# Reordering the prologue of a fused attention and two-layer MoE kernel: loads, scores, value sums and first copies

## The chip, the cores and the metric

The kernel runs on one core of a Trainium2 chip. The metric is the device time of one execution in microseconds (us). Three executions of the kernel before took 1382.09, 1383.53 and 1384.44 us; their median, 1383.53 us, is what the changed kernel is compared with. One more execution was recorded by the profiler.

## The reference

Attention with pooled keys and values feeds a dense feed-forward layer with ELU, and that feeds a layer of eight experts of which each token takes one.

```python
k_p = k.reshape(B, H, Sp, pool, D).mean(axis=3)          # B=8, H=8, S=576, D=64, pool=8, Sp=72
v_p = v.reshape(B, H, Sp, pool, D).mean(axis=3)
scores = q @ k_p.T / sqrt(D);  attn = softmax(scores);  x = attn @ v_p      # 4608 tokens x 512
h = x @ w_in;  g = where(h > 0, h, exp(min(h, 0)) - 1);  x = g @ w_out      # 512 -> 2048 -> 512
e = argmax(x @ w_gate);  out = softmax weight * relu(x @ w1[e]) @ w2[e]     # 8 experts, F = 1024
```

## The kernel before, in words

The 4608 tokens are 36 tiles of 128, three tiles to a block, twelve blocks. `first_block` (L867) is the prologue: it makes the attention output of tiles 0 to 2 (block 0). After it comes a list of steps, `step` (L836), one for each block and each of 16 slices of the hidden layer: 12 matmuls of the first product (`g1_mm`, L500, into tile `h`), the ELU on ScalarE and VectorE, and nine matmuls of the second product (`g2`, L540) of two steps earlier. The first steps also prepare tiles 3 to 5 and batch 1's keys (`k_sum`, L352, 40 small matmuls in step 0), and decode the weights.

For one tile t the prologue does this:

- `a_load` (L388) loads the queries `qT`; `s_mm` (L396) writes the scores of four heads into each of two PSUM banks (32 recorded matmuls);
- `s_max` and `s_exp` (L416, L421): VectorE takes the negative maxima `mx`, ScalarE the exponentials, eight per tile, each followed by a read of its accumulated sum `sm`;
- `s_norm` (L428): three VectorE instructions that scale the exponentials `s`;
- `t_mm` (L456): 16 recorded transposes on TensorE into two banks `aTp`; `t_copy` (L466) copies each bank to SBUF as `aT`;
- `pv_mm` (L472): 16 recorded matmuls of `aT` with the pooled values `v`; `pv_copy` (L483) writes the high part `xh` on ScalarE and the low part `xl` on VectorE, and both read the bank.

The pooled values of batch 0 come from `v_sum` (L338): five parts of the loaded values `natv`, two recorded matmuls each, accumulated in one bank, which `v_sum_copy` (L349) copies to `v` on ScalarE. A weight piece (n, c) is loaded by `w_load` (L183), multiplied by `w_mul` (L207), completed by the three VectorE instructions of `w_bits` (L222), and split by `w_hi` (ScalarE, L241) and `w_lo` (VectorE, L244). `warm(n)` (L288) issues n matmuls on zeros whose result nobody reads.

The order on every engine and on SP's DMA queue is the order of the program text, because the prologue and the steps stand inside a manual schedule (L953). PSUM banks are handed out in turn: `bank` (L279) gives alternately one of three banks `y` and one of three banks `a`. So the scores of tiles 0, 1 and 2 take y0/a0, y1/a1, y2/a2; the transposes of tile 0 take y0/a0, those of tile 1 y1/a1; `pv_mm(0)` takes y2, the transposes of tile 2 a2/y0, `pv_mm(1)` a0, `s_mm(3)` y1/a1, and `pv_mm(2)` takes y2 again. A bank is free for its next writer when its last reader is done. `v_sum(0)` and `warm` use two other banks, `h`.

The order of the prologue before, on the three compute engines, from the scores on:

- TensorE: scores 0, warm 6, scores 1, warm 6, scores 2, value parts 0 and 1, transposes 0, parts 2 and 3, transposes 1, part 4, `pv_mm(0)`, transposes 2, `pv_mm(1)`, scores 3, `pv_mm(2)`, step 0.
- ScalarE: exponentials 0, 1, 2, `w_hi(0,0)`, the two copies of `aT` 0, the copy of `v`, the two copies of `aT` 1, `xh` 0, `w_hi(0,1)`, one copy of `aT` 2, `xh` 1, `xh` 2.
- VectorE: maxima 0, `w_mul(0,0)`, maxima 1, `w_bits(0,0)`, maxima 2, `s_norm(0)`, `w_mul(0,1)`, `s_norm(1)`, `s_norm(2)`, `w_bits(0,1)`, `xl` 0, one copy of `aT` 2, `w_lo(0,0)`, `xl` 1, `w_lo(0,1)`, `xl` 2, maxima 3.

Of the kernel before, what the change touches and what calls it, by code (L numbers as in the profile page):

```python
# [97 lines left out]
def fused_kernel(ctx: ExitStack, tc: tile.TileContext, q, k, v, w_in, w_out, w_gate, w1, w2, cst, out):  # L98
    nc = tc.nc
# [83 lines left out]
    def w_load(n, c):  # L183
        kind, i = W_ORDER[n][0], int(W_ORDER[n][1])
        if n < len(W_ORDER) - 1:
            raw = w_tile([P, 512, 2], U32, f"raw{n}_{c}")
        elif c == 0:
            raw = mrpool.tile([P, 512, 2], U32, tag="yr", name=f"raw{n}_{c}")
        else:
            r = (2 * i + c) * P  # L190
            raws[n, c] = []
            for x in range(2):
                t = wgb_tile(f"raw{n}_{c}_{x}").bitcast(U32)
                nc.sync.dma_start(t, wov[r:r + P, 512 * x:512 * (x + 1)])
                raws[n, c].append((slice(256 * x, 256 * (x + 1)), t.rearrange("p (f t) -> p f t", t=2)))
            return
        if kind == "i":
            nc.sync.dma_start(
                raw.rearrange("p (c f) t -> p c (f t)", c=2),
                wiv[2 * c * P:2 * (c + 1) * P, 4 * i * P:4 * (i + 1) * P].rearrange("(c p) f -> p c f", p=P),  # L200
            )
        else:
            r = (2 * i + c) * P
            nc.sync.dma_start(raw.rearrange("p f t -> p (f t)"), wov[r:r + P, :])
        raws[n, c] = [(slice(0, 512), raw)]

    def w_mul(n, c, eng=None):  # L207
        if c == 0:
            kind, i = W_ORDER[n][0], int(W_ORDER[n][1])
            shape = [P, KC, 2 * P] if kind == "i" else [P, 2, DM]  # L210
            (wi if kind == "i" else wo)[i] = [
                w_tile(shape, F32R, f"w{kind}{x}{i}") for x in "hl"
            ]
        if n < 12:
            t = w_tile([P, 512], U32, f"dec{n}_{c}")
        else:
            t = spool.tile([P, S], U32, tag="st", name=f"dec{n}_{c}")[:, :512]
        decs[n, c] = t
        for q, r in raws[n, c]:
            (eng or nc.scalar.mul)(t.bitcast(F32)[:, q], r[:, :, 1].bitcast(F32), 2.0 ** -112)  # L220

    def w_bits(n, c):  # L222
        t = decs[n, c]
        raw = raws.pop((n, c))
        nc.vector.tensor_scalar(t, t, 3, None, op0=ALU.logical_shift_left)  # L225
        for q, r in raw:
            nc.vector.scalar_tensor_tensor(  # L227
                t[:, q], r[:, :, 1], 0x80000000, t[:, q], op0=ALU.bitwise_and, op1=ALU.bitwise_or
            )
        for q, r in raw:  # L230
            nc.vector.scalar_tensor_tensor(  # L231
                t[:, q], r[:, :, 0], 29, t[:, q], op0=ALU.logical_shift_right, op1=ALU.bitwise_or
            )
        if n < len(W_ORDER) - 1:
            w_free(f"raw{n}_{c}")
# [52 lines left out]
    def warm(n):  # L288
        ps = bank_h([P, 512], "warm")
        for _ in range(n):  # L290
            nc.tensor.matmul(ps, ones, zeros, start=True, stop=True)
# [32 lines left out]
    def n_load(b, kind):  # L324
        src = (k if kind == "k" else v)[b].rearrange("(s f) -> s f", f=DM)
        ts = []
        for x in range(2):
            t = w_tile([P, 2, DM], F32, f"nat{kind}{b}_{x}")
            nc.sync.dma_start(t, src[2 * P * x:2 * P * (x + 1), :].rearrange("(c p) f -> p c f", p=P))
            ts += [t[:, 0], t[:, 1]]  # L330
        t = w_tile([S - 4 * P, DM], F32, f"nat{kind}{b}_2")
        nc.sync.dma_start(t, src[4 * P:S, :])
        nats[b, kind] = ts + [t]
# [4 lines left out]
    def v_sum(b, parts):  # L338
        if 0 in parts:
            banks["vs", b] = bank_h([P, DM], f"vsum{b}") if b == 0 else bank([P, DM], f"vsum{b}")  # L340
        ps = banks["vs", b]
        for i in parts:
            t = nats[b, "v"][i]
            n, c = t.shape[0], SUM_AT - P // POOLW * i
            nc.tensor.matmul(ps[:SP], sums[:n, c:c + SP], t, start=i == 0, stop=i == 4)  # L345
        if 4 in parts:
            n_free(b, "v")
# [40 lines left out]
    def a_load(t):  # L388
        if t < 6:
            st = w_tile([P, 4, P], F32, f"qT{t}")  # L390
        else:
            st = ring(apool, [P, 4, P], F32, "qT", 2, f"qT{t}")
        nc.sync.dma_start(st, q[t])
        qTs[t] = st

    def s_mm(t):  # L396
        ss[t] = (
            wide["s"][:, :H * SP].rearrange("p (h s) -> p h s", h=H) if t >= T_TURN else work([P, H, SP], "s", f"s{t}"),
            ring(apool, [P, H], F32, "mx", 3, f"mx{t}"),
            ring(apool, [P, H], F32, "sm", 3, f"sm{t}"),  # L400
        )
        ps = [bank([P, 4, SP], f"sp{t}_{o}") for o in range(2)]
        qT = qTs.pop(t)
        for pr in range(4):
            for q in range(2):
                b = (P * t + HQ * q) // S
                qs = slice(HQ * q, HQ * (q + 1))
                for o in range(2):
                    os = slice(D * o, D * (o + 1))
                    nc.tensor.matmul(ps[o][qs, pr], qT[os, pr, qs], kTs[b % 2][os, pr], start=True, stop=True)  # L410
        for o in range(2):
            banks["s", t, o] = ps[o]
        if t < 6:
            w_free(f"qT{t}")
# [13 lines left out]
    def s_norm(t):  # L428
        s, _, sm = ss[t]
        nc.vector.tensor_scalar(sm, sm, 1e-9, float(POOLW), op0=ALU.add, op1=ALU.mult)  # L430
        nc.vector.reciprocal(sm, sm)
        nc.vector.tensor_mul(s, s, sm.unsqueeze(2).to_broadcast([P, H, SP]))
# [23 lines left out]
    def t_mm(t):  # L456
        s = ss[t][0]
        pss = [bank([P, H, HQ], f"aTp{t}_{q}") for q in range(2)]
        for h in range(H):
            for q in range(2):  # L460
                qs = slice(HQ * q, HQ * (q + 1))
                nc.tensor.transpose(pss[q][:SP, h], s[qs, h], ident[qs, qs])
        for q in range(2):
            banks["t", t, q] = pss[q]
# [402 lines left out]
    def first_block():  # L867
        warm(N_WARM)
        for pr in range(4):
            k_load(0, pr)  # L870
        a_load(0)
        a_load(1)
        for c in range(2):
            w_load(0, c)
        a_load(2)
        nc.sync.dma_start(ident, cst[:, C_ID:C_ID + P])
        nc.sync.dma_start(sums, cst[:, C_SUM:C_ALL])
        n_load(0, "v")
        a_load(3)
        for c in range(2):  # L880
            w_load(1, c)
        n_load(1, "k")
        for c in range(2):
            w_load(2, c)

        def exps(t):
            for hh in range(2):
                s_exp(t, hh)

        def maxs(t):  # L890
            for hh in range(2):
                s_max(t, hh)

        for pr in range(4):
            prep_k(0, pr)
        k_scale(0)
        v_tile(0)
        a_load(4)
        n_load(1, "v")
        s_mm(0)  # L900
        warm(6)
        maxs(0)
        exps(0)
        w_mul(0, 0, nc.vector.tensor_scalar_mul)
        s_mm(1)
        warm(6)
        maxs(1)
        exps(1)
        w_bits(0, 0)
        s_mm(2)  # L910
        v_sum(0, range(2))
        maxs(2)
        exps(2)
        a_load(5)
        s_norm(0)
        t_mm(0)
        v_sum(0, range(2, 4))
        w_hi(0, 0)
        t_copy(0, 0, nc.scalar.copy)
        t_copy(0, 1, nc.scalar.copy)  # L920
        w_mul(0, 1, nc.vector.tensor_scalar_mul)
        s_norm(1)
        t_mm(1)
        v_sum(0, range(4, 5))
        v_sum_copy(0)
        s_norm(2)
        pv_mm(0)
        t_mm(2)
        t_copy(1, 0, nc.scalar.copy)
        t_copy(1, 1, nc.scalar.copy)  # L930
        w_bits(0, 1)
        pv_copy(0)
        w_hi(0, 1)
        pv_mm(1)
        s_mm(3)
        t_copy(2, 0, nc.scalar.copy)
        t_copy(2, 1, nc.vector.tensor_copy)
        w_lo(0, 0)
        pv_copy(1)
        pv_mm(2)  # L940
        w_lo(0, 1)
        pv_copy(2)
        w_free("zeros")
        maxs(3)
        for c in range(2):
            w_load(3, c)
        nc.sync.dma_start(small, cst[:, C_W:C_END])
        load_small()
        for c in range(2):
            w_mul(1, c)  # L950
        copy_small()
# [630 lines left out]
```

## Time and profile before

| what | value |
|---|---|
| median of three executions | 1383.53 us (1382.09 to 1384.44) |
| the profiled execution, its own time | 1385.67 us |
| its span, first to last instruction | 1383.8 us |
| TensorE matmuls busy | 1357.7 us, 98% of the span |
| VectorE, ScalarE, GpSimd busy | 983.7, 772.1, 199.2 us |
| mean granted clock of TensorE | 0.993 of full speed |
| DMA moved | 169.41 MB |

The profiled execution is 2.14 us above the median of the other three, and 1.87 us of its own time lie outside the span. All starts are counted from the first instruction of the span. A busy share of TensorE counts matmuls whose ends are modelled, so full does not mean at its peak.

### The profile page before, as it was taken

To read this page: it belongs to the slowest core of one execution; us is meant where nothing else is said; L and a number is where in the kernel's file an instruction comes from. 1 tells how busy PE (TensorE), PEld (TensorE's weight loads), DVE (VectorE), ACT (ScalarE), POOL (GpSimd) and SP (SyncE) were. 2 spreads that over 40 slices of the span, in tenths; PEclk is the share of its full clock that TensorE was granted. 3 is DMA by queue.
4 is the path that set the end of the run, shared out by engine and by line. 5 is a ranking of instruction groups with operands and counts; after the bars stand their busy time and mean duration, and the time that the engine had idled before them with its cause. 6 is when DMAs were issued, how large, how long until landed. Compare 5 with 4: busy or idle time off the path is not lost.

```text
span 1383.8 us, 23759 instructions
## 1 busy us (share of the span) xinstructions
PE 1357.7 (98%) x8481; PEld 1164.8 (84%) x8482; DVE 983.7 (71%) x2395; ACT 772.1 (56%) x1889; POOL 199.2 (14%) x208
## 2 busy tenths in 40 slices
PE   8999999999999999999999999999999999999996
PEld 5798788888888888888889898988888887878785
DVE  7899979988878878787979786976556533335260
ACT  6777766666667676766666665642333333234251
POOL 0011011101211211111210000111121112112020
PEclk9999999999999999999999999999999999999998
DMA  9157434647353553545561522765664465759360
GB/s 348 62 174 211 134 69 108 69 82 71 76 81 63 93 57 76 68 65 83 73 91 39 63 39 46 160 109 174 137 117 159 145 217 194 259 180 338 129 217 22
DMA packets 109143, 169.41 MB, mean 122 GB/s; under 512 B 15509, under 2 KB 53015, under 8 KB 109016
## 3 DMA queue, kind: packets, MB, share of 16 engines
q1 hardware_dynamic: 91528, 135.45, 39.6%
q0 software_dynamic: 17488, 32.37, 12.0%
q8 instruction: 68, 1.11, 0.4%
q14 instruction: 59, 0.48, 0.2%
HBM read 146.35 MB, written 21.88 MB: 122 GB/s over the span
## 4 chain that ended last, share of the span: by engine, by line
PE 85%; DVE 5%; issue 5%; ACT 3%; DMA 1%; POOL 0%; SPq 0%; POOLq 0%; ACTq 0%; DVEq 0%
PE h L506 25%; PE y L548 25%; PE mhD L1212 13%; PE myD L1247 13%; PE pv L479 2%; PE sp L410 1%; PE zTD L1142 1%; DVE dec L227 1%; DVE dec L231 1%; ACT gh L530 1%; DVE junk L599 1%; PE mhT L1212 1%; ACT dec L220 1%; PE vsum L345 1%; DVE dec L225 1%
## 5 line engine op out<-in xcount | busy, mean ns | idle before, releaser
L548 PE MATMUL y<-woh,gh 128*128 128x512 f32 x576 | 230.6, 400 | 6.4 <-DVE yr L562 2.3
L548 PE MATMUL y<-wol,gh 128*128 128x512 f32 x576 | 226.6, 393 | 0.0
L548 PE MATMUL y<-woh,gl 128*128 128x512 f32 x576 | 226.5, 393 | 0.0
L599 DVE SCALAR_TENSOR_TENSOR junk<-yr,wgb 128x512 bf16<-128x512 f32 x264 | 180.7, 684 | 4.2 <-ACT yr L564 1.3
L506 PE MATMUL h<-xh,wih 128*128 128x384 f32 x768 | 168.5, 341 | 1.5 <-ACT xh L492 1.5
L530 ACT CAST gh<-g 128x384 fp32r<-128x384 f32 x192 | 98.6, 514 | 125.9 <-DVE g L524 107.1
L506 PE MATMUL h<-xl,wih 128*128 128x384 f32 x768 | 166.8, 338 | 0.0
L506 PE MATMUL h<-xh,wil 128*128 128x384 f32 x768 | 165.3, 336 | 0.0
L1225 DVE SCALAR_TENSOR_TENSOR hlD<-mhD,hhD 128x512 fp32r<-128x512 f32 x64 | 44.2, 690 | 161.5 <-ACT hhD L1224 153.5
L523 DVE SCALAR_TENSOR_TENSOR g<-g,th 128x384 f32<-128x384 f32 x192 | 106.3, 554 | 74.0 <-ACT th L518 73.8
L506 PEld LDWEIGHTS h<-xh,wih 128*128 128x128 f32 x768 | 139.3, 189 | 18.0 <-ACT xh L492 2.0
L1224 ACT ACTIVATE hhD<-mhD 128x512 fp32r<-128x512 f32 x64 | 38.4, 601 | 199.3 <-PE myD L1247 183.9
L516 ACT ACTIVATE th<-h 128x384 f32<-128x384 f32 x192 | 94.1, 490 | 96.0 <-PE h L506 95.2
L506 PEld LDWEIGHTS h<-xl,wih 128*128 128x128 f32 x768 | 137.9, 189 | 0.2
L506 PEld LDWEIGHTS h<-xh,wil 128*128 128x128 f32 x768 | 137.2, 188 | 0.0
L548 PEld LDWEIGHTS y<-woh,gh 128*128 128x128 f32 x576 | 108.1, 188 | 28.0 <-issue 2.8
L548 PEld LDWEIGHTS y<-woh,gl 128*128 128x128 f32 x576 | 108.3, 188 | 24.0
L531 DVE TENSOR_TENSOR gl<-g,gh 128x384 fp32r<-128x384 f32 x192 | 106.8, 556 | 23.5 <-ACT gh L530 20.1
L548 PEld LDWEIGHTS y<-wol,gh 128*128 128x128 f32 x576 | 108.3, 188 | 16.2
L524 DVE TENSOR_TENSOR g<-g,h 128x384 f32<-128x384 f32 x192 | 106.3, 554 | 6.6
L518 ACT ACTIVATE th<-th 128x384 f32<-128x384 f32 x192 | 100.9, 525 | 6.1
L517 ACT ACTIVATE g<-th 128x384 f32<-128x384 f32 x192 | 100.8, 525 | 6.1
(282 smaller groups left out, 2346.3 us busy)
## 6 DMA issues: line engine op xcount, KB each, us to landing
wgb<-in_moe_w_gate_dram SPq DMA_DIRECT2D x96, 256.0 KB
w1stD<-in_moe_w_dram SPq DMA_DIRECT2D x32, 512.0 KB
w2stD<-in_moe_w_dram SPq DMA_DIRECT2D x32, 512.0 KB
qT<-in_q_dram SPq DMA_DIRECT2D x36, 256.0 KB
ybuf<-yr SPq DMA_DIRECT2D x33, 256.5 KB
raw<-in_moe_w_in_dram SPq DMA_DIRECT2D x16, 512.0 KB
raw<-in_moe_w_out_dram SPq DMA_DIRECT2D x15, 512.0 KB
t1U<-in_moe_w_dram SPq DMA_DIRECT2D x12, 512.0 KB
```

The costliest lines, as they stand in the source:

```text
L506: mark["g1"] = nc.tensor.matmul(ps, wi[i][a][:, c, o:o + P], bb[blk][:, c, :], start=n == 0, stop=n == 3 * KC - 1).ins
L516: nc.scalar.activation(th, hps[blk, f], AF.Relu, scale=-1.0)
L517: nc.scalar.activation(g, th, AF.Exp, scale=-1.0)
L518: nc.scalar.activation(th, th, AF.Tanh, scale=-0.5)
L523: nc.vector.scalar_tensor_tensor(g, g, 1.0, th, op0=ALU.add, op1=ALU.mult)
L524: nc.vector.tensor_max(g, g, hps.pop((blk, f)))
L530: nc.scalar.copy(gh, g)
L531: nc.vector.tensor_sub(gl, g, gh)
L548: nc.tensor.matmul(ys[blk][j], a[:, js], wo[i][bb][:, o, :], start=n == 0 and f in FIRST[blk], stop=n == 2 and f in LAST[blk],)
L599: nc.vector.scalar_tensor_tensor(junk, yrows[blk][j][:, :DM], 1.0, pes[blk, e], op0=ALU.mult, op1=ALU.mult, accum_out=lgs[blk][:, j, e:e + 1])
L1212: mark["g1"] = nc.tensor.matmul(ps[:, x], a[:, c, o * P:(o + 1) * P], y[:, c], start=k == 0, stop=k == len(terms) - 1).ins
L1247: nc.tensor.matmul(yps[it][u], a[:, us], second[w][:, o], start=i == 0 and o == 0 and n == 0, stop=i == 3 and o == 1 and n == 2,)
```

## The change

Only `first_block` is edited. On SP's queue the queries of tile 2, the two small constants and the values of batch 0 are issued before the first two weight pieces instead of after them. On TensorE the scores of the three tiles stand in a row, then eight warming matmuls (twelve before), then the transposes of tile 0 and all five value parts in a row. On ScalarE the copies of `aT` 0 and of `v` stand between the exponentials of tile 1 and those of tile 2. On VectorE the first weight decode stands behind `s_norm(1)`, and `w_bits(0,1)` directly behind `s_norm(2)`, ahead of the copy of `aT` 2.

```diff
         for pr in range(4):
             k_load(0, pr)
-        a_load(0)
-        a_load(1)
-        for c in range(2):
-            w_load(0, c)
-        a_load(2)
+        for t in range(3):
+            a_load(t)
         nc.sync.dma_start(ident, cst[:, C_ID:C_ID + P])
         nc.sync.dma_start(sums, cst[:, C_SUM:C_ALL])
         n_load(0, "v")
+        for c in range(2):
+            w_load(0, c)
         a_load(3)
...
         a_load(4)
         n_load(1, "v")
-        s_mm(0)
-        warm(6)
-        maxs(0)
-        exps(0)
-        w_mul(0, 0, nc.vector.tensor_scalar_mul)
-        s_mm(1)
-        warm(6)
-        maxs(1)
-        exps(1)
-        w_bits(0, 0)
-        s_mm(2)
-        v_sum(0, range(2))
-        maxs(2)
+        for t in range(3):
+            s_mm(t)
+            maxs(t)
+            if t < 2:
+                exps(t)
+        warm(8)
+        s_norm(0)
+        t_mm(0)
+        v_sum(0, range(5))
+        for hh in range(2):
+            t_copy(0, hh, nc.scalar.copy)
+        v_sum_copy(0)
         exps(2)
         a_load(5)
-        s_norm(0)
-        t_mm(0)
-        v_sum(0, range(2, 4))
-        w_hi(0, 0)
-        t_copy(0, 0, nc.scalar.copy)
-        t_copy(0, 1, nc.scalar.copy)
-        w_mul(0, 1, nc.vector.tensor_scalar_mul)
         s_norm(1)
         t_mm(1)
-        v_sum(0, range(4, 5))
-        v_sum_copy(0)
+        pv_mm(0)
+        w_mul(0, 0, nc.vector.tensor_scalar_mul)
+        w_bits(0, 0)
+        for hh in range(2):
+            t_copy(1, hh, nc.scalar.copy)
+        w_mul(0, 1, nc.vector.tensor_scalar_mul)
         s_norm(2)
-        pv_mm(0)
         t_mm(2)
-        t_copy(1, 0, nc.scalar.copy)
-        t_copy(1, 1, nc.scalar.copy)
         w_bits(0, 1)
+        w_hi(0, 0)
+        t_copy(2, 0, nc.scalar.copy)
+        t_copy(2, 1, nc.vector.tensor_copy)
         pv_copy(0)
-        w_hi(0, 1)
         pv_mm(1)
         s_mm(3)
-        t_copy(2, 0, nc.scalar.copy)
-        t_copy(2, 1, nc.vector.tensor_copy)
-        w_lo(0, 0)
+        w_hi(0, 1)
         pv_copy(1)
         pv_mm(2)
+        w_lo(0, 0)
+        pv_copy(2)
         w_lo(0, 1)
-        pv_copy(2)
         w_free("zeros")
```

## Rows read from the trace of the kernel before

**Rows 1.** Busy by stretch: bounds, length, then each engine's, PEclk, DMA share, GB/s.

```profile
7.00:25.00 18.00, 15.48 (x249) 8.57 (x248) 13.57 (x31) 13.11 (x60) 0.00 (x0) 1.00 1.05 380
60.00:1300.00 1240.00, 1232.31 (x7444) 1065.38 (x7443) 906.04 (x2261) 703.73 (x1704) 187.19 (x192) 1.00 0.53 117
```

**Rows 2.** Chain that ended last, start to 100 us: start, length, what.

```profile
6.77 6.24 DMA natv<-in_v_dram
13.15 1.91 PE vsum L345 x4
15.32 0.64 PE aTp L462 x16
...
18.40 0.88 PE vsum L345 x2
19.30 0.59 ACT v L350
19.93 1.09 PE pv L479 x16
...
22.62 0.66 PE sp L410 x32
...
24.36 0.59 ACT xh L492
24.99 2.38 PE h L506 x12
27.38 6.27 PE ksum L358 x40
33.64 3.61 PE h L506 x12
```

**Rows 3.** Timeline of ScalarE in the prologue: start, length, instruction, idle before.

```profile
9.21 0.32 ACT L426 ACTIVATE s<-sp,mx 128x72 f32<-128x72 f32 x1 [7.18 <-DVE mx L417]
...
11.49 0.24 ACT L426 ACTIVATION_READ_ACCUMULATOR s<-sp,mx 128x1 f32 x1
11.58 0.36 ACT L426 ACTIVATE s<-sp,mx 128x72 f32<-128x72 f32 x1
...
16.81 1.15 ACT L470 COPY aT<-aTp 72x512 f32<-72x512 f32 x2
...
19.30 0.58 ACT L350 COPY v<-vsum 72x512 f32<-72x512 f32 x1 [1.34 <-PE vsum L345]
```

**Rows 4.** Timeline of VectorE in the prologue.

```profile
14.03 0.16 DVE L430 TENSOR_SCALAR sm<-sm 128x8 f32<-128x8 f32 x1
...
14.46 0.76 DVE L432 TENSOR_TENSOR s<-s,sm 128x576 f32<-128x576 f32 x1
...
17.71 0.42 DVE L225 TENSOR_SCALAR dec<-dec 128x512 uint32<-128x512 uint32 x1
...
18.89 0.69 DVE L231 SCALAR_TENSOR_TENSOR dec<-raw,dec 128x512 uint32<-128x512 uint32 x1
...
22.30 0.68 DVE L470 COPY aT<-aTp 72x512 f32<-72x512 f32 x1
22.90 0.68 DVE L245 TENSOR_TENSOR wil<-dec,wih 128x512 fp32r<-128x512 f32 x1
```

**Rows 5.** Timeline, step 1: ScalarE and VectorE waiting for TensorE.

```profile
37.33 0.49 ACT L516 ACTIVATE th<-h 128x384 f32<-128x384 f32 x1 [2.09 <-PE h L506]
...
37.88 0.69 DVE L470 COPY aT<-aTp 72x512 f32<-72x512 f32 x1 [1.20 <-PE aTp L462]
```

**Rows 6.** Busy by stretch where TensorE's clock falls (columns of rows 1).

```profile
28.00:29.00 1.00, 1.00 (x11) 1.00 (x11) 0.47 (x3) 1.00 (x6) 0.00 (x0) 1.00 1.01 324
...
30.00:31.00 1.00, 1.00 (x6) 1.00 (x7) 0.79 (x2) 0.65 (x2) 0.00 (x0) 0.50 1.02 385
...
275.60:279.00 3.40, 1.99 (x7) 1.37 (x8) 3.25 (x9) 2.60 (x6) 0.00 (x0) 0.97 0.07 10
279.00:282.40 3.40, 3.40 (x11) 3.12 (x11) 2.61 (x10) 0.62 (x2) 0.00 (x0) 0.53 0.84 193
```

## The prediction, written before the changed kernel was run

> **What bounds the kernel now.** I read the busy table by stretch first: from 60 to 1300 us TensorE's matmuls are busy 1232.31 of 1240.00 us [rows 1]. The reader is to see that nothing behind the prologue can take up a delay or spoil a gain on TensorE: whatever moves the start of that stretch moves the end by as much. The edit lies wholly ahead of it, so I read the chain of waits from the start [rows 2]. It runs through the landing of the values at 13.01 us (6.77 + 6.24), then over TensorE almost without a break: value parts, transposes, the copy of `v` at 19.30, `pv_mm(0)` at 19.93, the last `xh` at 24.36, step 0 at 24.99. Then come step 0's 12 matmuls (2.38), `k_sum` (6.27) and step 1's 12 matmuls at 33.64. In step 1 ScalarE waits 2.09 us for the product and VectorE 1.20 us for transposes [rows 5], so TensorE leads there and lateness of the other two up to those sizes is hidden. The number to work out is the new start of step 0.
>
> **Loads.** The values move ahead of two weight pieces of 524,288 bytes; at 380 GB/s [rows 1] they land 2.8 us sooner, an estimate of 10.2 us for the first pair in place of 13.01. This buys nothing: the value parts now stand behind the transposes of tile 0, which can't start before 13.05 us (below). Had the move no effect at all, the cost would still be nil, as 13.01 is before that. The queries of tile 2 come sooner and the first weights later, by the 1.18 MB of values, 0.26 MB of queries and 0.13 MB of constants now ahead of them: 1.57 MB or 4 us, so they land some 13 to 15 us, and their first user `w_mul(0,0)` now stands behind `s_norm(1)` at about 15.3. Cover: if that is 1 us late, only `w_bits(0,0)` shifts, which has until `w_hi(0,0)` at 22. Everything behind these on SP's queue has the same bytes ahead of it as before. I cost the loads at 0, between 0 and +0.5.
>
> **Scores and warming.** Three sets of scores, 0.66 each [rows 2], and eight warming matmuls now fill TensorE from 7.9 to about 11.9 us, where the trace of before has twelve. Nothing waits for them: ScalarE needs only maxima 0 to begin at 9.21 [rows 3], as before. Cost 0. The clock is granted at 1.00 from 7 to 25 us already [rows 1]. The Trainium skill's Perfetto Trace Analysis, section Matmul Optimizations, advises back-to-back batches because the engine scales its power with utilization. By that rule the batches would be a gain; the row shows full clock throughout, so the sum by the rule is the same as by the row, and the rule bites only where this order makes new gaps (the forecast's clock term).
>
> **Value sums in a row, copies between exponentials.** This is the part that costs. Step by step:
>
> 1. Exponentials 0 run from 9.21, those of tile 1 from 11.58: 2.37 us a tile. The last sum of tile 0 is read at 11.73 [rows 3].
> 2. `s_norm` takes 14.03 to 15.22, 1.19 us, and the transposes begin 0.10 later [rows 2, 4]. So `s_norm(0)` ends at 12.95 and the transposes of tile 0 run 13.05 to 13.69 (0.64).
> 3. Ten value matmuls now follow. Two bursts of four at 1.91 and one of two at 0.88 make 4.70 at most [rows 2]; in one burst the drained ends in between fall away, so I take 4.5. They end at 18.2, against 19.28 before (18.40 + 0.88): 1.1 us sooner.
> 4. ScalarE finishes exponentials 1 at 13.95 and the two copies of `aT` 0 (1.15) at 15.1. Its next instruction is the copy of `v`, which waits for TensorE until 18.2. Queued behind it are exponentials 2. Before, the same copy waited 1.34 us with nothing urgent behind it [rows 3]; now ScalarE stands still for 3.1 us in front of 2.37 us of work on the path. Exponentials 2 run from about 18.7 to 21.2; before, all three sets had ended at about 16.4 (9.21 + 3 x 2.37 + the last read).
> 5. `pv_mm(0)` has its operands at 18.8, but its bank y2 holds scores 2 until the first half of exponentials 2 is done: about 20.0. It runs to 21.1 (1.09); before it began at 19.93.
> 6. `s_norm(2)`: 21.2 to 22.4; transposes 2: 22.5 to 23.1.
> 7. On VectorE `w_bits(0,1)` comes next, 17.71 to 19.58 before, 1.87 us [rows 4]: to 24.2. Then its half of `aT` 2 and `xl` 0, issued 0.60 apart (22.30, 22.90) and 0.68 long [rows 4]: `xl` 0 ends at 25.4.
> 8. TensorE: `pv_mm(1)` 23.1 to 24.1, scores 3 to 24.8. `pv_mm(2)` needs y2, which `xl` 0 frees at 25.4: 25.45 to 26.5. `xh` 2 takes 0.59, and step 0 begins at **27.2**, 2.2 us later than 24.99.
>
> VectorE's own tail (`xl` 2, `w_lo(0,1)`, maxima 3) shifts by about 2.8 us, 0.6 more than TensorE; the 1.20 us of [rows 5] covers it, and without that cover it would cost 0.6. The last half of the low weights comes at about 28.4, where step 0 asks for it (27.2 + 1.4).
>
> **The clock.** The new order leaves TensorE work of some 1.1 us (`pv_mm(0)`) between 18.8 and 22.5, with gaps of about 1.2 and 1.4 us. No row of before shows that stretch, so bounds. Below: the clock holds, 0. The nearest row is 275.60 to 279.00, where TensorE is busy 1.99 of 3.40 us, after which the clock is granted at 0.53 over 279.00 to 282.40, half speed for nearly all of it [rows 6]; the new stretch is emptier. It also fell to 0.50 (the 1.2 GHz level) during `k_sum`'s small matmuls, 11 a microsecond at 28 and 6 at 30 [rows 6], 1.8 times slower. I take the nearest row: it falls near 23. `pv_mm(1)` and scores 3, 1.7 us, then take 3.1, less the 0.7 they would have waited for y2: +0.7; part of `pv_mm(2)` +0.3 to +0.8. I take +1.0. Above: step 0's matmuls at half clock too, 1.2 more (3.61, partly slow, against 2.38 [rows 2]), and the first part of `k_sum`, 1.5: +3.7 in all.
>
> **Sum.** 0 for the loads, +2.2 for the held exponentials, +1.0 for the clock: +3.2. The profiled execution's own 1385.67 (span 1383.8 and 1.87 around it) would become 1388.9; it stands 2.14 above the median, to which I move the sum: 1383.53 + 3.2 = **1386.7 us**, slower by 0.23%. A difference of about 0.2%, 2.8 us, is what a measurement of this kernel can tell from none.
>
> **Rivals.**
>
> - *The clock holds (0.30).* Not slower by what can be told: +2.2, 1385.7. The mechanism is the grant between 18.8 and 25 us; it decides from the point where the gaps are too short to lower it. For it: before, 7 to 25 us passed at full clock though 2.5 of 18 us were idle [rows 1]. Against it: 275.60 to 279.00 [rows 6]. Some executions may fall and others hold; then the median lies between.
> - *The fall moves out of `k_sum` (0.14).* If step 0's dense matmuls lift the clock later than before, `k_sum` runs at 11 a microsecond: 40 in 3.6 instead of 6.27, and step 1 in 2.38 instead of 3.61: 3.9 us back. With the +2.2 that is -1.7, 1381.8; in part, 1382 to 1384.5. For it: 3.9 us of low clock are there to win. Against: `k_sum` itself is what lowered it.
> - *The copies slip in as the edit's order means them to (0.08).* If value sums ended by 15.1, exponentials 2 would run on to 18.2, transposes 2 by 20, and step 0 would begin near 23.8: -1.2, 1382.3, and with the previous rival's gain faster than 1380.8. Against it: value sums stand behind transposes 0 on TensorE and 4.5 us don't fit between 13.69 and 15.1. The early landing would do what it is placed for only if TensorE took the sums first, and the order is fixed.
>
> **How the numbers follow.** Forecast (held exponentials and a clock that falls) 0.48, the rivals 0.30, 0.14, 0.08. The forecast alone spans 1385.3 to 1389.0 (clock term 0.4 to 3.7, within errors). The range takes in the holding clock and the upper part of the moved fall, and leaves out most of the last two cases: 1383.2 to 1389.0. Slower than 1386.3: six tenths of the forecast, a third of the first rival, a little for errors: 0.43. Faster than 1380.8: 0.06, from the last two together. Within: 0.51, although the likeliest single case lies just outside it.
>
> **What would show it.** ScalarE idle about 3.1 us ahead of the copy of `v`, released by TensorE's value sums at 18.2; exponentials 2 from 18.7; TensorE idle over 1 us ahead of `pv_mm(0)`, released by ScalarE's exponentials, and again ahead of transposes 2; `pv_mm(2)` released by VectorE's `xl`; step 0 near 27.2 or 28.2; a granted clock of 0.5 somewhere from 21 to 27 us if the clock term is right. Wrong: exponentials 2 beginning near 15, or step 0 before 25, or step 0 late by 2 us while step 4 is not.

## The result, and the profile after

The changed kernel takes 1390.85 us (median of 7 executions, 1388.14 to 1395.04) beside 1384.44 us for the kernel before (7 executions). The ratio is 1.0054, with a 95% interval of 1.0040 to 1.0068: slower by 7.5 us, with 5.5 to 9.4 as ends; the medians lie 6.4 us apart. The forecast was slower by 3.2 us, and its range ended at 1389.0.

The profiled execution took 1389.68 us, against 1385.67 before. Where its time came from is seen first on ScalarE. The timeline of the changed kernel, with the lines of [rows 3] in their new places:

```profile
13.74 1.08 ACT L470 COPY aT<-aTp 72x512 f32<-72x512 f32 x2
18.35 0.58 ACT L350 COPY v<-vsum 72x512 f32<-72x512 f32 x1 [3.53 <-PE vsum L345]
18.83 0.32 ACT L426 ACTIVATE s<-sp,mx 128x72 f32<-128x72 f32 x1
...
21.21 1.08 ACT L470 COPY aT<-aTp 72x512 f32<-72x512 f32 x2
```

The copy of `v` waits 3.53 us (1.34 before), and exponentials 2 stand behind it: they run from 18.83 to 21.2. TensorE's timeline shows what that leaves, and answers to [rows 2] (the first fence is the changed kernel, the second rows of before that the text compares with):

```profile
12.99 0.73 PE L462 MATMUL aTp<-ident,s 64*72 64x64 f32 x16 [1.73 <-DVE s L432]
13.65 4.23 PE L345 MATMUL vsum<-natv,sums 128*72 128x512 f32 x9
...
20.19 1.09 PE L479 MATMUL pv<-aT,v 72*64 72x128 f32 x16 [1.43 <-ACT s L426]
22.72 0.99 PE L462 MATMUL aTp<-ident,s 64*72 64x64 f32 x16 [1.43 <-DVE s L432]
23.64 1.97 PE L479 MATMUL pv<-aT,v 72*64 72x128 f32 x16
25.54 1.24 PE L410 MATMUL sp<-kT,qT 64*64 64x72 f32 x32
26.71 1.98 PE L479 MATMUL pv<-aT,v 72*64 72x128 f32 x16
29.37 1.65 PE L506 MATMUL h<-xh,wih 128*128 128x384 f32 x4 [0.69 <-ACT xh L492]
...
33.26 5.68 PE L358 MATMUL ksum<-sums,natk 128*128 128x16 f32 x40
38.87 1.65 PE L506 MATMUL h<-xh,wih 128*128 128x384 f32 x4
```

```profile
22.55 0.73 PE L410 MATMUL sp<-kT,qT 64*64 64x72 f32 x32
...
27.21 6.43 PE L358 MATMUL ksum<-sums,natk 128*128 128x16 f32 x40
33.57 1.65 PE L506 MATMUL h<-xh,wih 128*128 128x384 f32 x4
```

`pv_mm(0)` and transposes 2 are each preceded by 1.43 us of idle TensorE, released by the exponentials and by `s_norm(2)`. From then on the same 16 matmuls of `pv_mm` take 1.97 in place of 1.09 us, and scores 3 take 1.24 in place of 0.73. Step 0 starts at 29.37, 4.38 later than before, and step 1 at 38.87 in place of 33.57. The busy table of the changed kernel by stretch gives the reason in its column PEclk (columns as in [rows 1]):

```profile
13.00:18.80 5.80, 5.76 (x42) 2.37 (x42) 3.62 (x8) 2.27 (x10) 0.00 (x0) 1.00 1.05 404
18.80:22.80 4.00, 1.18 (x19) 0.97 (x21) 1.36 (x4) 4.00 (x20) 0.00 (x0) 1.00 1.04 376
22.80:25.00 2.20, 2.20 (x30) 2.04 (x31) 2.13 (x5) 1.34 (x4) 0.00 (x0) 0.51 1.04 407
25.00:29.37 4.37, 3.69 (x54) 2.81 (x51) 1.86 (x4) 1.48 (x4) 0.00 (x0) 0.50 1.05 374
29.37:33.20 3.83, 3.83 (x12) 3.83 (x13) 3.72 (x7) 3.18 (x17) 0.59 (x1) 0.51 1.05 394
33.20:36.50 3.30, 3.30 (x32) 3.30 (x31) 2.44 (x6) 2.53 (x9) 0.26 (x2) 1.00 0.89 290
36.50:43.00 6.50, 6.50 (x24) 6.01 (x23) 4.92 (x9) 2.42 (x5) 0.00 (x0) 0.50 0.61 218
```

After a stretch with 1.18 us of matmuls in 4.00 the granted clock falls to 0.5, the 1.2 GHz level, and stays there through the rest of the prologue and nearly all of step 0, until about 33.1. `k_sum` then runs for more than half of its time at full clock, and step 1 at half. In the prologue and first steps of before, only `k_sum` and step 1 met a low clock, from after 29 us [rows 6].

One row of each kernel measures the whole prologue: the ScalarE instruction that starts the ELU of step 4, behind which TensorE hardly waits any more. Kernel before, then changed kernel:

```profile
61.96 0.49 ACT L516 ACTIVATE th<-h 128x384 f32<-128x384 f32 x1 [2.53 <-PE h L506]
```

```profile
67.82 0.49 ACT L516 ACTIVATE th<-h 128x384 f32<-128x384 f32 x1 [2.54 <-PE h L506]
```

The shift is 5.86 us. Below, "the shift" is this row's start less 61.96. The line numbers in the profiles are those of the kernel before.

The whole profiled execution grew by less, 4.01 us. The shift holds until the changed kernel reaches the work of the row 275.60 to 279.00 of before [rows 6], behind which the clock of before fell to 0.53. In the changed kernel's profile the same work, 6.0 us later, is followed by full clock (columns as in [rows 1]), and the next ELU (before, then changed) comes only 4.74 us later:

```profile
281.60:285.00 3.40, 1.96 (x7) 1.34 (x8) 3.25 (x9) 2.62 (x6) 0.00 (x0) 1.00 0.08 9
285.00:288.40 3.40, 3.40 (x28) 3.02 (x29) 2.61 (x10) 0.80 (x3) 0.00 (x0) 1.00 0.26 98
```

```profile
283.39 0.49 ACT L516 ACTIVATE th<-h 128x384 f32<-128x384 f32 x1 [1.19 <-PE h L506]
```

```profile
288.13 0.49 ACT L516 ACTIVATE th<-h 128x384 f32<-128x384 f32 x1
```

So each profile has its own falls of the clock, and one pair of profiles tells a difference to one or two us only. For every execution the mean granted clock over its whole span is known too: 0.987 to 0.991 in the thirteen executions of the changed kernel (this result and experiment 10), and 0.993 or 0.994 in the median of those of before beside the experiments, with a few at 0.990 or 0.991.

### The profile page after: what moved, and what is told of

It reads as the page before. It is cut to its first block, busy times and chain, and to the rows that moved or that the text cites. A ratio compares the mean times of both kernels' runs of the same rounds, so it can differ in the third digit from the quotient of the medians.

```text
span 1387.9 us, 23753 instructions
## 1 busy us (share of the span) xinstructions
PE 1360.5 (98%) x8478; PEld 1167.4 (84%) x8478; DVE 984.5 (71%) x2395; ACT 772.3 (56%) x1889; POOL 200.4 (14%) x208
```

## The experiments

All times are medians beside executions of the kernel before on the same chip (medians 1384.2 to 1384.6).

**1. The order of the exponentials undone in the changed kernel.**

```diff
         for t in range(3):
             s_mm(t)
             maxs(t)
-            if t < 2:
-                exps(t)
+            exps(t)
...
         v_sum_copy(0)
-        exps(2)
         a_load(5)
```

> The changed kernel with one edit undone: the exponentials of tile 2 stand directly behind those of tile 1 again, ahead of the copies of aT 0 and of v; loads, scores in a row, eight warming matmuls, value sums in a row and VectorE's order stay. Theory (the held exponentials are the cause, and the low clock follows from TensorE's gaps behind them): exponentials 2 run 13.7 to 16.1, pv_mm(0) starts near 18.9 in place of 20.2, the clock stays at 1.00 until k_sum, step 0 starts near 24 (24.99 before, 29.37 changed), time about 1383.5, not slower than before. Rival A (fewer warming matmuls and the idle TensorE from 11.3 to 13.0 lower the clock): the clock still falls near 23 and step 0 starts after 27, time 1388 or more. Rival B (the loads or VectorE's order): step 0 stays later than 26.5.

Measured: 1384.4 us (12 executions), ratio 0.9995 (0.9985 to 1.0005): the whole loss is gone. The loads, the eight warming matmuls, the row of value sums and VectorE's order, all still as changed, together cost nothing that can be told. But the profiled execution (1387.27 us, the slowest of the twelve; shift 1.37, step 0 at 26.37 where the theory had it near 24) shows a thing the theory had denied. The busy table of this kernel around the stretch in which TensorE waits for the first `s_norm`:

```profile
11.50:13.30 1.80, 0.13 (x1) 0.00 (x0) 1.13 (x3) 1.80 (x14) 0.00 (x0) 1.00 1.06 322
...
14.60:18.00 3.40, 3.40 (x6) 0.97 (x5) 3.26 (x7) 2.97 (x16) 0.00 (x0) 0.50 1.06 408
```

Here the clock fell to 0.50 at the value sums, which took 5.93 us in place of 4.23. So the idle stretch at 11.3 to 13.0, which the change makes by giving up the spread warming matmuls, can lower the clock too, as rival A had it, in some executions.

**2. The changed kernel with TensorE's two gaps filled.**

```diff
         t_mm(1)
+        warm(6)
         pv_mm(0)
+        warm(6)
```

> The changed kernel plus twelve more warming matmuls on TensorE, six ahead of pv_mm(0) and six behind it, into the two gaps of 1.43 us that wait for the exponentials of tile 2; nothing else is moved, so the exponentials are held as in the changed kernel. Theory (stall and clock are two costs): the clock holds at 1.00 until k_sum, pv_mm(1) takes about 1.0 us as before, step 0 starts near 27.2, the first ELU of step 4 comes 2.2 to 2.5 us later than the 61.96 of before in place of 5.86, time about 1386.7. Rival (the gaps are not what lowers the clock, or the low clock costs little): step 0 still at 29 and time 1390 to 1391.

Measured: 1388.22 us (11 executions, one of them 1396.64), ratio 1.0029 (1.0014 to 1.0045); shift 2.72. The profile is nearly as the theory said, the time 1.5 us above it. Its TensorE timeline:

```profile
20.47 1.09 PE L479 MATMUL pv<-aT,v 72*64 72x128 f32 x16
21.50 1.47 PE L291 MATMUL warm<-zeros,ones 128*128 128x512 bf16 x6
22.99 0.64 PE L462 MATMUL aTp<-ident,s 64*72 64x64 f32 x16
23.57 1.09 PE L479 MATMUL pv<-aT,v 72*64 72x128 f32 x16
...
25.89 1.09 PE L479 MATMUL pv<-aT,v 72*64 72x128 f32 x16 [0.57 <-DVE xl L493]
27.67 0.97 PE L506 MATMUL h<-xh,wih 128*128 128x384 f32 x4 [0.68 <-ACT xh L492]
```

Twelve matmuls that compute nothing bring `pv_mm` back to 1.09 us, step 0 to 27.67 and the shift from 5.86 to 2.72: they change nothing but what TensorE does while it waits. Three of the eleven executions, 1396.64 among them, record a mean clock of 0.991, as low as the changed kernel's best; the others 0.992 to 0.994.

**3. The held exponentials alone, in the kernel before.**

```diff
         maxs(2)
-        exps(2)
         a_load(5)
...
-        w_hi(0, 0)
         t_copy(0, 0, nc.scalar.copy)
...
         v_sum_copy(0)
+        exps(2)
+        w_hi(0, 0)
         s_norm(2)
```

> The kernel before with one edit: the exponentials of tile 2 (and the w_hi(0,0) that followed them) stand behind the copies of aT 0 and of v; loads, warming, split value sums stay as before. Theory: the copy of v waits for the value sums until 19.3, exponentials 2 run 19.8 to 22.2, pv_mm(0) starts near 21.2, step 0 no sooner than 28.3, and TensorE's gaps lower the clock as in the changed kernel: 1389 to 1392. Rival (the scores, sums and loads together are the cause, not this order alone): about 1384.4, step 0 near 25.

Measured: 1392.71 us (6 executions), ratio 1.0055 (1.0042 to 1.0069), shift 6.87. The clock is at 0.63 from 23 to 28 and at 0.50 from 28 to 33, step 0 starts at 30.41, and `pv_mm(0)` waits for the exponentials:

```profile
21.44 1.09 PE L479 MATMUL pv<-aT,v 72*64 72x128 f32 x16 [1.88 <-ACT s L426]
```

The place of one tile's exponentials in ScalarE's order (with the `w_hi` that follows them) makes a loss as large as the change's, with nothing else of the change present. It is a little larger in the profile, as the value sums, still split, end later here.

**4. The loads alone, in the kernel before.**

```diff
-        a_load(0)
-        a_load(1)
-        for c in range(2):
-            w_load(0, c)
-        a_load(2)
+        for t in range(3):
+            a_load(t)
...
         n_load(0, "v")
+        for c in range(2):
+            w_load(0, c)
         a_load(3)
```

> The kernel before with the order of the loads alone changed: queries 2, the constants and the values of batch 0 ahead of the first two weight pieces. Theory: the value sums no longer wait for their data at 13.15 but follow scores 2 at 12.8, and w_mul(0,0), which stands ahead of maxima 1 on VectorE here, waits for its weights until about 13.4; that holds maxima 1 and so the exponentials of tile 1, which could have begun at 11.6: 2 us of ScalarE, so step 0 at 26 to 27 and 1385 to 1388. It says that the load order is free only together with the moved decode. Rival (the loads alone explain the changed kernel's time through the bandwidth they share): 1390 or more with no wait of VectorE for the weights.

Measured: 1389.34 us (12 executions), ratio 1.0032 (1.0021 to 1.0042), shift 5.00, step 0 at 30.59. The mechanism is the theory's, the size is beyond it. VectorE's timeline:

```profile
8.75 0.82 DVE L417 TENSOR_REDUCE mx<-sp 128x4 f32<-128x288 f32 x2 [1.10 <-PE sp L410]
14.38 0.43 DVE L220 TENSOR_SCALAR dec<-raw 128x512 f32<-128x512 f32 x1 [4.81 <-DMA raw<-in_moe_w_in_dram]
14.72 0.82 DVE L417 TENSOR_REDUCE mx<-sp 128x4 f32<-128x288 f32 x2
```

The first decode gets its weights at 14.38 us, not at 13.4, and maxima 1 wait behind it; ScalarE then idles 3.44 us. TensorE idles 4.57 us ahead of transposes 0, and behind that the clock was low for a while here too (0.66 from 18 to 23): value parts 2 and 3 took 3.36 us in place of 1.94. So the load order isn't free without the moved decode, which the change has.

**5. The held exponentials with all three gaps filled.** Experiment 2 with fifteen in place of eight warming matmuls ahead of transposes 0:

```diff
-        warm(8)
+        warm(15)
```

> The changed kernel with its exponentials of tile 2 held as they are, but TensorE given warming matmuls in all three idle stretches: fifteen in place of eight ahead of the transposes of tile 0, and six on either side of pv_mm(0). Theory (the wait costs 2.2 to 2.8 us by itself; the rest of the change's loss is low clock, and the second experiment's time above its profile's shift came from executions whose clock fell after the gap at 11.3 to 13.0): clock at 1.00 until k_sum, first ELU of step 4 at 64.2 to 64.8, time 1386.6 to 1387.4, spread no wider than that of before. Rival (warming matmuls don't save it; the held exponentials cost more than 3 us even at full clock): 1388.5 or more.

Measured: 1388.66 us (12 executions), ratio 1.0021 (1.0009 to 1.0034), shift 2.86. By the ratio that is 2.9 us, by the profile 2.86; the median, 1388.66, lies above the 1387.4 expected, where the rival had it, and the spread (1384.47 to 1392.07) isn't narrower. The busy table of this kernel shows full clock until `k_sum` begins, and TensorE busy where it had idled:

```profile
18.00:23.00 5.00, 4.92 (x44) 1.00 1.05 368
23.00:28.00 5.00, 3.72 (x82) 1.00 1.05 383
28.00:33.00 5.00, 5.00 (x37) 0.95 1.04 374
```

(Here the columns are TensorE's busy time and count, PEclk, DMA share, GB/s.) So the wait by itself costs about 2.9 us, 1.2 to 4.7 by the ratio's interval; by the medians it is 4.4, and the rival's "more than 3 us" isn't refuted. Two of the twelve executions, 1390.04 and 1392.07, record a mean clock of 0.990 and the others 0.992 to 0.994, so the clock seems not to have held in all of them. Filling the gap at 11.3 us as well gained nothing over experiment 2, against the theory.

**6. Value sums ahead of transposes 0, in the kernel of experiment 1.**

```diff
-        t_mm(0)
-        v_sum(0, range(5))
+        v_sum(0, range(5))
+        t_mm(0)
```

> The first experiment's kernel (exponentials 2 directly behind 1) with the five value parts ahead of the transposes of tile 0 on TensorE, so that the early landing of the values is used. Theory: value sums run from about 11.3 to 15.7 with no gap ahead of them, the transposes of tiles 0 and 1 follow, exponentials end at 16.1, the copy of v comes behind those of aT 0 at about 17.5 and waits for nothing, pv_mm(0) starts near 18.1 (21.05 in the first experiment's profile, 19.93 before), step 0 near 23.5; 1382.5 to 1383.5, ratio below 1 by 0.05 to 0.15%. Rival (TensorE is led by something else in the prologue, as the weights' decode): step 0 no sooner than 24.5, 1384 to 1385.

Measured: 1387.13 us (12 executions), ratio 1.0014 (1.0001 to 1.0027), shift 2.04: a miss. All until `pv_mm(0)` came as expected (17.98), but TensorE idled 1.19 us ahead of it after two sets of transposes, and the clock fell again:

```profile
17.98 1.09 PE L479 MATMUL pv<-aT,v 72*64 72x128 f32 x16 [1.19 <-ACT v L350]
19.20 0.64 PE L462 MATMUL aTp<-ident,s 64*72 64x64 f32 x16
19.77 1.91 PE L479 MATMUL pv<-aT,v 72*64 72x128 f32 x16
...
25.44 1.65 PE L506 MATMUL h<-xh,wih 128*128 128x384 f32 x4 [0.69 <-ACT xh L492]
```

An order whose attention work is earlier on every engine up to 18 us is slower at the end, and its rows show the slow matmuls from `pv_mm(1)` on: neither theory nor rival had named that. The executions' mean clocks point to the same cause: seven with 0.989 to 0.991 took 1387.10 to 1390.27 us, five with 0.992 to 0.995 took 1382.90 to 1385.70. Where the clock held, the order seems to have done about what the theory said.

**7. Experiment 1 with the gap at 11.3 us filled.**

```diff
-        warm(8)
+        warm(15)
```

> The first experiment's kernel with fifteen warming matmuls ahead of the transposes of tile 0 in place of eight, so that TensorE isn't idle from 11.3 to 13.0. Theory (the fall at 14.63 in the first experiment's profile came from that gap, and cost its value sums 1.7 us): no fall before k_sum, value sums 4.2 us in place of 5.9, step 0 near 24.4, median about 1383.5. Rival (that gap has nothing to do with it): a fall near 14 to 18 again, or the median stays at 1384.4 with a step 0 near 24.4.

Measured: 1384.28 us (12 executions), ratio 1.0000 (0.9990 to 1.0009), shift -1.57. The profile has no fall ahead of `k_sum`, the value sums take 4.23 us and step 0 starts at 24.81, 0.18 us sooner than in the kernel before; most of the rest of the shift is `k_sum`, 4.62 us in place of 6.43. The median is where the rival put it: 0.1 us from experiment 1's. That gap lowers the clock in some executions, as the first experiment's profile shows, but it doesn't decide the median.

**8. A version meant to beat both.** Loads, scores in a row and the moved decode stay, and the exponentials of all three tiles stand in a row, as in experiment 1. Then comes this order (the program text, with cuts):

```python
        warm(4)
        v_sum(0, range(5))
        s_norm(0)
        t_mm(0)
        s_norm(1)
        t_mm(1)
        warm(6)
        for hh in range(2):
            t_copy(0, hh, nc.scalar.copy)
        v_sum_copy(0)
...
        pv_mm(0)
        for hh in range(2):
            t_copy(1, hh, nc.scalar.copy)
        s_norm(2)
        t_mm(2)
        w_mul(0, 1, nc.vector.tensor_scalar_mul)
        pv_copy(0)
        for hh in range(2):
            t_copy(2, hh, nc.scalar.copy)
        w_bits(0, 1)
```

> A version meant to be faster than both: loads, moved decode and scores in a row as changed; exponentials of the three tiles in a row; four warming matmuls, the five value parts, the transposes of tiles 0 and 1, six warming matmuls; then copies of aT 0, of v, pv_mm(0), with xh 0 and xl 0 ahead of the copies of aT 2 (both on ScalarE) and of w_bits(0,1). Theory: no engine waits long, clock at 1.00 until k_sum, pv_mm(0) near 17.7, step 0 at 23.0 (24.99 before), 1382.0 to 1383.0, about 0.1 to 0.15% faster than before. Rival (k_sum's low clock decides: what is won ahead of step 0 is lost or doubled by where the clock falls): profile shift at step 0 of -2, but a median anywhere from 1381 to 1385.

Measured: 1382.63 us (12 executions), ratio 0.9985 (0.9975 to 0.9995), shift -3.02: faster than both kernels, against the one before by 2.1 us by the ratio and 1.6 by the medians. Its ScalarE and TensorE timelines:

```profile
16.38 1.13 ACT L470 COPY aT<-aTp 72x512 f32<-72x512 f32 x2
17.33 0.67 ACT L350 COPY v<-vsum 72x512 f32<-72x512 f32 x1
17.80 1.16 ACT L470 COPY aT<-aTp 72x512 f32<-72x512 f32 x2
```

```profile
16.48 1.47 PE L291 MATMUL warm<-zeros,ones 128*128 128x512 bf16 x5
18.05 1.09 PE L479 MATMUL pv<-aT,v 72*64 72x128 f32 x16
...
23.48 0.96 PE L506 MATMUL h<-xh,wih 128*128 128x384 f32 x4 [1.06 <-ACT xh L492]
...
25.71 4.62 PE L358 MATMUL ksum<-sums,natk 128*128 128x16 f32 x40
```

The copy of `v` waits for nothing, since its sums ended long before, and no exponential stands behind it. `pv_mm(0)` starts when it did in experiment 6, but six warming matmuls stand in the gap ahead of it, and no later `pv_mm` is slow. Step 0 starts 1.51 us sooner than before; the rest of the shift comes mostly from `k_sum`, which ran at full clock in this execution (4.62 in place of 6.43 us), as the rival had allowed. Several orders differ from experiment 6 at once, so the part of each isn't shown.

**9. VectorE's order, priced at full clock.** Experiment 5 with

```diff
+        w_bits(0, 1)
         s_norm(2)
         t_mm(2)
-        w_bits(0, 1)
```

> The fifth experiment's kernel (exponentials 2 held, TensorE kept busy with warming matmuls) with w_bits(0,1) ahead of s_norm(2) on VectorE, where that engine waits 3.6 us for the exponentials in the changed kernel's profile. Theory (of the held exponentials' 2.8 us, about 0.5 is xl 0 standing behind w_bits(0,1), which keeps pv_mm(2) from its bank): xl 0 ends near 25.5 in place of 26.0, pv_mm(2) no longer idles 0.57 us, first ELU of step 4 about 0.4 us sooner than in the fifth, 64.4; time 0.4 us below the fifth's, which is at the edge of what can be told. Rival (that bank wait is hidden by xh on ScalarE): step 4 as in the fifth, 64.8.

Measured: 1386.44 us (11 executions), ratio 1.0014 (1.0004 to 1.0023). `pv_mm(2)` idles 0.16 in place of 0.57 us and step 0 starts at 27.36 in place of 27.85: the 0.5 us are there. The shift, 0.83, fell by 2.03, more than this edit explains: in this execution the low clock of `k_sum` and step 1 was shorter (PEclk 0.66 from 33 to 38, against 0.50 in experiment 5), so the rest isn't the edit's.

**10. The changed kernel once more.**

> The changed kernel once more, for another profiled execution beside the first one and more times on the same chip as the ninth. Theory (the order fixes the gaps, and where the clock falls and rises around them differs from execution to execution): exponentials 2 again begin within 0.2 us of the copy of v's start plus 0.5, pv_mm(0) again idles about 1.4 us; the low clock begins anywhere from 20 to 25 us and lasts until 30 or later; step 4's shift between 4 and 9 us; times spread over 1388 to 1395. Rival (the order of execution sets the clock's moments exactly): the same two low stretches, 22.9 to 33.1 and 36.5 to 43.3, within 0.3 us, and step 4's shift 5.9.

Measured: 1392.26 us (6 executions), ratio 1.0060 (1.0044 to 1.0076); in its profile the copy of `v` waits 3.53 us again, both gaps are 1.43 us again, `pv_mm(1)` takes 1.97 us, and PEclk is 0.98 from 18 to 23 and 0.50 from 23 to 33. The shift is 6.46. Both low stretches begin and end within 0.2 us of the first profile's, at 22.9 to 33.1 and 36.5 to 43.3, though TensorE's work from the scores to step 0 comes some 0.7 us later here (`pv_mm(0)` at 20.87). So for this pair the rival was right on the clock, and the larger shift fits that later start.

## Why the prediction was right or wrong

**Bound.** Right for the median: the shift is 5.86 us, and the median moved by 6.4. The profiled pair ended only 4.01 us apart, mostly through the fall at 279 us that the profile of before has and the changed kernel's hasn't.

**Loads, scores and warming at nothing.** Right for the change as a whole: experiment 1 keeps them all and stands at ratio 0.9995. The cover named for the weights was needed: without the moved decode the same loads cost 5.00 us of shift (experiment 4). The cost 0 for fewer warming matmuls hid a risk, seen in one profile of experiment 1 and not in its median.

**The held exponentials, +2.2.** Right in mechanism, and low in size by 0.5 to 0.7 us in the profiles. The steps came within 0.2 to 0.3 us of their forecasts: value sums ended near 18.3 (18.2), exponentials 2 started at 18.83 (18.7), `pv_mm(0)` at 20.19 (20.0), transposes 2 at 22.72 (22.5). With the clock held, step 0 came at 27.67 and 27.85 (27.2), shifts of 2.72 and 2.86; by times the two cost 2.9 to 4.4 us. Undoing this one order takes away all of the loss, and doing it alone makes as large a one (experiments 1 and 3). The VectorE part of it, `xl` 0 behind `w_bits(0,1)`, is 0.5 us (experiment 9).

**The clock, +1.0.** This is the step that failed: "I take +1.0", between 0 and +3.7. That it would fall near 23 was right. The row it was judged by, the gaps of 275.60 to 279.00 [rows 6], was a weaker guide than I took it for: the same work in the changed kernel's profile was followed by full clock. The size was wrong. I let it recover within the prologue, so that it slowed only `pv_mm(1)`, scores 3 and part of `pv_mm(2)`. It stayed at 0.50 through nearly all of step 0, whose first four matmuls took 1.65 us against 0.97 at full clock in experiment 2, and step 1 ran at half clock as well. Of the 5.86 us, the held order with a held clock is 2.86 (experiment 5), so the clock is 3.0, three times what I took and inside the bounds that I had written down. Between these two profiles it is 1.5 us ahead of step 0, 1.7 in step 0 (3.89 us to the start of `k_sum`, against 2.21), 0.6 in step 1, and 0.8 given back in `k_sum`. The first was at the top of what I had worked out for the prologue; step 0 I had put into the upper bound alone, at 1.2. The first exponentials start at 8.96 in the one profile and 9.42 in the other, which leaves some 0.5 us of doubt.

By the ratios the clock's share is larger, outside my bounds: 1.0054 less 1.0021 is 0.0033 of 1384, 4.6 us. By the medians it is smaller, 6.4 less 4.4. Each way it is at least twice the 1.0. The two profiled executions of the changed kernel, 1389.68 and 1390.20, are below their medians, so the others lost more than the profiles show. In the first set the clock has a part in it: the three shortest executions record a mean of 0.990, the four longest 0.988 or 0.989. Experiment 10's six don't sort that way, and where the low clock lay in the longer ones stays open.

**The range.** It ended at 1389.0, below the sum of the upper bounds that stood in the same text: 1383.53 + 2.2 + 3.7 = 1389.4, and the loads' +0.5 besides. The half-clock term should have been carried through whatever dense work followed, by the one row of a dense step at low clock that was there, 3.61 against 2.38 [rows 2]. Even with the loads' part the bounds end at 1389.9, below 1390.85: another 0.9 us is the kernel before, whose seven executions have 1384.44 as median, where the forecast started from 1383.53.

**The rivals.** *The clock holds*: refuted in both profiles of the changed kernel, and by the mean clocks of its executions; experiments 2 and 5 show what it would have been, ratio 1.0021 to 1.0029. *The fall moves out of `k_sum`*: in small part: `k_sum` took 5.68 in place of 6.43 us, but steps 0 and 1 lost more than that. Its price was also read wrongly: I divided 40 by the 11 a microsecond of a single row and got 3.6 us, but where `k_sum` ran wholly at full clock it took 4.62 (experiments 7, 8 and 9). *The copies slip in*: no, and for the reason given; experiment 8 has the sums ahead of the transposes and no exponential behind the copy, and is faster; experiment 6 has both too, and its median is not, as its clock fell in most executions.

**The batches.** The Trainium skill's Perfetto Trace Analysis, Matmul Optimizations, asks for back-to-back batches, for the sake of the engine's scaled power. The runs agree, in the sense that counts here: experiments 2, 5 and 8 fill gaps with work that computes nothing, and in their profiles the matmuls behind them run at full clock until `k_sum`.

## What to carry to other kernels

On an engine that works in program order, a copy that waits should have nothing of the critical chain queued behind it; look at what stands behind the waiting instruction before asking what the copy releases. Price a gap on TensorE twice: the wait itself, and the granted clock of everything dense that follows it; here the second was about as large as the first. Where a gap can't be closed, matmuls that compute nothing and write to a spare bank can be worth their slots.

## What the runs showed of the hardware that was not expected

- A low clock outlasted work: from 22.72 to 28.69 us TensorE's matmuls followed each other without a gap, at 0.50 from 22.9 on, and the 12 dense matmuls of step 0 from 29.37 on still ran at 0.51; it was granted 1.00 again only near their end.
- The price of half clock, which the trace of before lacked for the small matmuls: 16 of `pv_mm` 1.97 against 1.09 us, 32 of the scores 1.24 against 0.73; four of the first product 1.65 against 0.97. The factor is 1.7 to 1.8 in these recorded lengths, not 2.
- A gap of 1.19 us ahead of `pv_mm(0)`, behind two sets of transposes, was followed by low clock (experiment 6; by the mean clocks in seven of its twelve executions), and 1.43 us twice likewise; with the gap at 11.3 to 13.0 us the clock fell in one profile (experiment 1) and held in three others (the changed kernel's two and experiment 2's).
- The same work can be followed by either clock: 1.99 of 3.40 us busy and then 0.53 in the profile of before, 1.96 of 3.40 and then 1.00 in the changed kernel's.
- The low stretches of two executions of the changed kernel agreed within 0.2 us while the work in them differed by some 0.7 us.
